# Softmax scalings and low parts of the early FFN from ScalarE and VectorE to GpSimd, with the weight pieces dealt out anew

## The chip, the cores and the metric

The kernel runs on one core of a Trainium2 chip. The metric is the device time of one execution in microseconds (us), as the median of several. The engines are named as in the profile: PE (TensorE, matrix products and transposes), PEld (its loading of weights), DVE (VectorE), ACT (ScalarE), POOL (GpSimd) and SP (SyncE, which only issues DMAs here).

## What is computed

Attention with a decay per key, 8 batches of 8 heads with 576 rows and 64 columns, and behind it a feed-forward network (FFN) on the 4608 × 512 output. All data are float32.

```python
def _attn_ref(q, k, v, f):
    scores = scale * np.matmul(q, k.transpose(0, 1, 3, 2))
    cum = np.cumsum(np.log(np.clip(f, 0.0001, 1.0)), axis=-1)
    decay = cum[:, :, :, None] - cum[:, :, None, :]
    scores = np.where(causal, -1000000000.0, scores + decay)
    attn = np.exp(scores - np.max(scores, axis=-1, keepdims=True))
    attn = attn / (np.sum(attn, axis=-1, keepdims=True) + 1e-09)
    return np.matmul(attn, v)

def _moe_ref(x, w_in, w_out):        # x: 4608 x 512, w_in: 512 x 2048, w_out: 2048 x 512
    h = x @ w_in
    return np.maximum(0.01 * h, h) @ w_out
```

## The kernel before

The large products are made of three: each operand is split into a high part in a rounded format that PE multiplies fast, and a low part, the rest; high by high, high by low and low by high are added up. So for the FFN the input has `xh` and `xl`, the weights `win_h`, `win_l`, `wout_h`, `wout_l`, and the activated hidden tile `g` has `gh` and `gl`.

The kernel has an early part and a main part. The **early part** (the loop over `steps`, some 140 us) handles the first 256 rows of three batches, 12 pairs of heads, four to a batch. At step x it issues, in this order: the loads of the next pair (`early_load`), the scores of pair x (`early_scores`), weight pieces up to the sum of `WQ[:x + 1]` (`load_weight`), the values of pair x − 1 (`early_values`), and so many quanta of the FFN as `FQ[x]` says (0 for the first four steps, then 4, then 8). The **main part** goes through the other rows head by head, with quanta of the FFN between its pieces; behind it the rest of the FFN runs alone.

*Scores of an early pair*: PE makes four score tiles `sce`, two of 128 and two of 256 columns. For each, DVE adds the causal mask and takes the maximum (L279, into `ze`), and ACT the exponential with the row sum (L283). Behind the last of them DVE prepares the reciprocal of the sums (L288, L289), and the four tiles are scaled by it (L291, an activation on ACT). *Values*: PE transposes `ze` (`tre`), ACT copies the result (`pte`, L303), PE multiplies with `ve` (`ave`), ACT writes `xh` (L316) and DVE `xl` (L317). The first FFN tile of a group of 256 rows needs `xh` and `xl` of all four pairs of its batch.

*A weight piece* (16 in all; even ones are two column blocks of `w_in`, odd ones of `w_out`) comes as packed 64-bit numbers: SP fetches it into `wraw` (L156; two buffers, so a fetch waits until the last step of the piece two before is done), ACT converts (L170), DVE shifts (L171), ACT rounds to the high part (L172), DVE masks, scales the rest, subtracts and adds (L173, L175, L179, L180), the last of which writes `win_l` or `wout_l`. Piece n is used by the FFN's column block n // 2.

*A quantum chain of the FFN* (`ffn`): 24 matmuls make `h` of 256 rows and 256 hidden columns, ACT makes `g` from it (L587), DVE `gh` (L590), and `gl` is `g − gh` (L592). In the main part POOL does `gl`, in the early part and in the last iteration DVE. In the next block's turn `second` multiplies `gh` and `gl` with `wout` into `o`. `qk`, `ve`, `g`, `gh` and `gl` share five buffers with the tag `b2`, so a new tile waits until the last reader of an older one is done.

The order of the instructions on each engine is fixed when the kernel is built: a scheduler takes the program's order and priorities and lays out one list for each engine, which the engine goes through in that order. So a change of the program can shift places in the lists of engines that it does not name.

Of the kernel before, what the change touches and what calls it, by code (L numbers as in the profile page):

```python
# [12 lines left out]
AF = mybir.ActivationFunctionType  # L13
ALU = mybir.AluOpType
# [8 lines left out]
B2 = 5  # L23
B4 = 4
NE = 3
WQ = (1, 1, 1, 1, 1, 1, 1, 1, 2, 2, 2, 2)
ZE = (("z0", "z1", "z2", "z3"), ("vm", "s2b", "m2b", "s2a"))
FQ = (0, 0, 0, 0, 4, 8, 8, 8, 8, 8, 8, 8, 8)
BUFS = dict(s1=2, m1=2, ost=2)
# [8 lines left out]
def forgetting_attention_ffn(ctx, tc, qT, kT, v4, vr, f, w_in, w_out, out):  # L38
# [6 lines left out]
    nc = tc.nc  # L45
# [23 lines left out]
    def width(i):  # L69
        return min((i + 1) * P, S)  # L70
# [32 lines left out]
    def matmul(*args, **kw):  # L103
        work[0] += 1
        nc.tensor.matmul(*args, **kw)  # L105
# [7 lines left out]
    def warm(n):  # L113

        ps = psum.tile([P, 512], F32, tag="h", name=f"warm_{len(warmed)}")
        warmed.append(n)
        for _ in range(n):
            matmul(ps, still[:, :P], still, start=True, stop=True)
# [66 lines left out]
    def weights(n):  # L185
        while len(loaded) < min(n, len(wpieces)):
            load_weight(len(loaded))
# [23 lines left out]
    for i in range(NCH):  # L211
        c = slice(i * P, width(i))
# [12 lines left out]
    def load(t):  # L225

        s, c0, c1 = tasks[t]
        h = state[t] = {}
        a, n = c0 * P, S
        for name, src, lo in (("q", qT, a), ("k", kT, 0)):  # L230
            x = h[name] = one.tile([P, S], F32, tag=f"{name}raw", name=f"{name}raw_{t}")
            for o in range(2):
                nc.sync.dma_start(x[o * D:(o + 1) * D, lo:n], src[s][:, lo:n])
        if s % 2 == 0:
            g = s // 2
            vm = fixed["vm"]
            nc.sync.dma_start(vm[:, :, :NFULL], v4[g])
            nc.sync.dma_start(vm[:REST, :, NFULL], vr[g])
            pairs[s // 2, c0] = {}
# [14 lines left out]
    def early_scores(b, g):  # L254
        e = early[b, g]
        mx = one.tile([P, 4], F32, tag="max", name=f"maxe_{b}_{g}", bufs=3)
        sm = one.tile([P, 4], F32, tag="sum", name=f"sume_{b}_{g}", bufs=3)
        for i in range(2):
            n = width(i)
            ps = [  # L260
                psum.tile([P, 512], F32, tag="sc", name=f"sce_{b}_{g}_{2 * o + i}")[:, :n]
                for o in range(2)
            ]
            for o in range(2):
                x = e["qk"][o * D:(o + 1) * D]
                matmul(ps[o], x[:, 0, i * P:n], x[:, 1, :n], start=True, stop=False)
            for o in range(2):
                s = b * HPB + 2 * g + o
                matmul(
                    ps[o], pick[:, s:s + 1].broadcast_to([P, P]), decay_r[i],  # L270
                    start=False, stop=True,
                )
            for o in range(2):
                c = 2 * o + i
                tag = ZE[g % 2][c]
                z = e[c] = one.tile(
                    [P, n], F32, tag=tag, name=f"ze_{b}_{g}_{c}", bufs=BUFS.get(tag, 1)
                )
                nc.vector.tensor_tensor_reduce(  # L279
                    out=z, in0=ps[o], in1=tri[:, TRI - n:], scale=-SCALE, scalar=3.0e38,  # L280
                    op0=ALU.add, op1=ALU.min, accum_out=mx[:, c:c + 1],
                )
                nc.scalar.activation(  # L283
                    z, z, AF.Exp, bias=mx[:, c:c + 1], scale=-1.0, accum_out=sm[:, c:c + 1]
                )
            if b * HPB // 2 + g < WARM[2]:
                warm(WARM[1])
        nc.vector.tensor_scalar(sm, sm, 1.0e-9, None, op0=ALU.add)  # L288
        nc.vector.reciprocal(sm, sm)  # L289
        for c in range(4):  # L290
            nc.scalar.activation(e[c], e[c], AF.Copy, scale=sm[:, c:c + 1])  # L291

    def early_values(b, g):
        e = early[b, g]
# [241 lines left out]
    since, done = {}, []  # L536
# [7 lines left out]
    def fetch_group(n):  # L544
        if n not in groups and n not in staged and (n + 1) * T <= ready[0]:
            xs = staged[n] = one.tile([P, NCC, T], F32R, tag="b4", name=f"xs_{n}", bufs=B4)
            since[n] = work[0]
            nc.sync.dma_start(xs.bitcast(F32), xd[:, n * T:(n + 1) * T].rearrange("(c p) t -> p c t", p=P))
# [8 lines left out]
    def ffn():  # L557
        pending = None
        half = NFC // 2
        order = [(0, 0, HP), (1, 0, HP), (0, HP, half), (1, HP, half)]  # L560
        order += [(n, 0, half) for n in range(2, NG)]
        for at, (n, p0, p1) in enumerate(order):
            while (n + 1) * T > ready[0]:
                yield False
            if n not in groups:
                if n not in staged:
                    fetch_group(n)
                while n not in groups:
                    yield False
            acc = [None, None]  # L570
            for p in range(p0, p1):
                while len(loaded) < 2 * (p + 1):
                    yield False
                xh, xl = groups[n]
                ph = psum.tile([P, 2, T], F32, tag="h", name=f"h_{n}_{p}")
                for e in range(2):
                    fs = slice(e * P, (e + 1) * P)
                    for c in range(NCC):
                        for x, (w, xx) in enumerate(((win_h[p], xh), (win_h[p], xl), (win_l[p], xh))):
                            matmul(  # L580
                                ph[:, e, :], w[:, c, fs], xx[:, c, :],
                                start=(c == 0 and x == 0), stop=(c == NCC - 1 and x == 2),
                            )
                    if e == 0:
                        yield True
                g = one.tile([P, 2, T], F32, tag="b2", name=f"g_{n}_{p}", bufs=B2)
                nc.scalar.activation(g, ph, AF.Prelu, alpha=0.01)  # L587
                gh = one.tile([P, 2, T], F32R, tag="b2", name=f"gh_{n}_{p}", bufs=B2)
                gl = one.tile([P, 2, T], F32R, tag="b2", name=f"gl_{n}_{p}", bufs=B2)
                nc.vector.tensor_copy(gh, g)  # L590
                eng = nc.gpsimd if heads[0] else nc.vector
                eng.tensor_tensor(gl, g, gh.bitcast(F32), op=ALU.subtract)  # L592
                yield True
                if pending is not None:
                    yield from second(*pending)
                if p0 < p and at + 1 < len(order):
                    fetch_group(order[at + 1][0])
                pending = (n, p, p0, p1, gh, gl, acc)
        yield from second(*pending)
# [27 lines left out]

    parts = {}
    quanta = ffn()
    heads = [False]  # L630
    ready, used, credit = [0], [0], [0.0]

    def fill(n):

        settle()
        credit[0] += n
        while credit[0] >= 1:
            credit[0] -= 1
            if not next(quanta, None):
                credit[0] = 0  # L640
                return
            used[0] += 1

    nt = len(tasks)
# [16 lines left out]
    for x, (b, g) in enumerate(steps + [(NE, 0)]):  # L661
        if x + 1 < len(steps):
            early_load(*steps[x + 1])
        if x < len(steps):
            early_scores(b, g)
            weights(sum(WQ[:x + 1]))
        if x:
# [5 lines left out]
    load(0)  # L673
    split(0)
    for t in range(nt + 1):
        heads[0] = t < nt
        if t + 1 < nt:
            load(t + 1)
        before = list(range(max(tasks[t - 1][1] - 1, 0), NCH)) if t else []
        now = list(range(*tasks[t][1:])) if t < nt else []  # L680
        have = ready[0] // T * NQ - used[0]
        left = min((e + 2 - t for e in ends if e + 1 >= t), default=1)
        step = min(have / (left + SLACK), MAXQ) / 8
        fill(step)
        for i in range(5):
            if i in before:
                transposes(t - 1, i)
            if i in now:
                scores(t, i)
            fill(step)  # L690
            if i == 1 and t and tasks[t - 1][0] % 2:
                inverse(t - 1)
        if t:
            for part in range(len(spans(t - 1))):
                values(t - 1, part)
                fill(step)
            if tasks[t - 1][0] % 2:
                normalise(t - 1)
            s, c0, c1 = tasks[t - 1]
            if s % HPB == HPB - 1:  # L700
                ready[0] = place[s // HPB, c0 * P] + S - c0 * P
        if t + 1 < nt:
            split(t + 1)
        fill(step * (3 - len(spans(t - 1)) if t else 1))
# [37 lines left out]
```

## Time and profile before

| what | value |
|---|---|
| time, median of 3 runs | 1215.92 us (1212.28 to 1219.12) |
| the profiled execution | 1216.96 us, span 1215.0 us, mean granted PE clock 0.993 |
| busy in the span | PE 1190.4 us (98%), DVE 623.4 (51%), ACT 628.6 (52%), POOL 467.9 (39%) |
| instructions | PE 7812, DVE 1682, ACT 1631, POOL 475 |

The profile shows one execution. Its rows give busy time and the idle time ahead of an instruction with what ended it. The span runs from the first to the last instruction; the time of the execution is 1.96 us longer. A group of instructions is shown as line, engine, operation, out<-in with the shapes, and their number; behind the bar stand the busy time and the mean ns of one, then the idle time before them and its releasers. In a timeline a row has start, duration, engine, line and operation; in brackets the idle time ahead and its releaser.

### The profile page before, as it was taken

How to read it: one execution, taken by the hardware profiler on the slowest of the kernel's cores; microseconds unless marked ns; L12 is line 12 of the kernel's file. 1: busy time of each engine (PE TensorE's matmuls, PEld its weight loads, DVE VectorE, ACT ScalarE, POOL GpSimd, SP SyncE). 2: the span in 40 equal slices, each digit the busy share in tenths (PEclk: the TensorE clock that was granted, in tenths of full speed). 3: DMA queues.
4: the chain of work that ended last, by engine and by line, in shares of the span. 5: the costliest groups of instructions: out<-in, count | busy, mean ns of one | idle time of the engine just before them, and what ended most of it. 6: DMA issues, size and time to landing. Idle time of an engine off the chain costs nothing.

```text
span 1215.0 us, 22228 instructions
## 1 busy us (share of the span) xinstructions
PE 1190.4 (98%) x7812; PEld 1070.4 (88%) x7812; DVE 623.4 (51%) x1682; ACT 628.6 (52%) x1631; POOL 467.9 (39%) x475
## 2 busy tenths in 40 slices
PE   8999989999999999999999999999999999999998
PEld 5678879888889999999999999999999999999997
DVE  6898556666645555455544444545444434553211
ACT  5876546667645565555545445454444444652111
POOL 2000255564455445454344453534454544531000
PEclk9899999999999999999999999999999999999999
DMA  6554233334333233323231322222223222211000
GB/s 193 168 192 165 83 103 110 95 104 140 107 106 97 79 97 97 114 80 92 83 109 51 89 80 90 73 90 61 75 84 90 60 69 81 72 57 47 18 18 18
DMA packets 81103, 110.53 MB, mean 91 GB/s; under 512 B 19616, under 2 KB 50704, under 8 KB 80992
## 3 DMA queue, kind: packets, MB, share of 16 engines
q1 hardware_dynamic: 80992, 109.11, 29.6%
q8 instruction: 62, 1.02, 0.3%
q14 instruction: 49, 0.40, 0.1%
HBM read 82.62 MB, written 18.58 MB: 83 GB/s over the span
## 4 chain that ended last, share of the span: by engine, by line
PE 86%; DVE 4%; ACT 3%; DMA 3%; issue 2%; POOL 1%; SPq 0%; ACTq 0%; POOLq 0%; DVEq 0%
PE h L105 32%; PE o L105 30%; PE tr L109 7%; PE av L105 7%; PE sc L105 7%; PE sce L105 1%; DMA kraw<-in_kT 1%; DMA wraw<-in_w_out 1%; ACT fixed_z L384 1%; PE ave L105 1%; DVE fixed_z L378 1%; DMA wraw<-in_w_in 1%; DVE pl L430 1%; DMA xd<-x 0%; DVE wraw L179 0%
## 5 line engine op out<-in xcount | busy, mean ns | idle before, releaser
L105 PE MATMUL h<-xh,win_h 128*128 128x256 f32 x1152 | 330.2, 287 | 0.3 <-ACT xh L316 0.3
L105 PE MATMUL h<-xh,win_l 128*128 128x256 f32 x1152 | 327.9, 285 | 0.0
L105 PE MATMUL h<-xs,win_h 128*128 128x256 f32 x1024 | 290.0, 283 | 4.0 <-POOL xs L143 4.0
L592 POOL TENSOR_TENSOR gl<-g,gh 128x512 fp32r<-128x512 f32 x111 | 146.9, 1324 | 290.9 <-DVE gh L590 269.0
L105 PE MATMUL o<-wout_h,gh 128*128 128x512 f32 x576 | 230.6, 400 | 0.0
L105 PE MATMUL o<-wout_l,gh 128*128 128x512 f32 x576 | 226.6, 393 | 0.0
L105 PE MATMUL o<-wout_h,gl 128*128 128x512 f32 x576 | 225.3, 392 | 0.0
L105 PEld LDWEIGHTS h<-xh,win_h 128*128 128x128 f32 x1152 | 220.7, 192 | 3.4 <-ACT xh L316 0.8
L105 PEld LDWEIGHTS h<-xh,win_l 128*128 128x128 f32 x1152 | 221.2, 192 | 0.7 <-issue 0.7
L384 ACT ACTIVATE fixed_z<-fixed_z,max 128x192 f32<-128x192 f32 (+3 forms) x272 | 161.0, 592 | 106.0 <-DVE max L378 102.4
L378 DVE CUSTOM_DVE_ANT_0 fixed_z<-sc,tri 128x192 f32<-128x192 f32 (+3 forms) x272 | 122.6, 452 | 159.3 <-PE sc L105 156.3
L105 PEld LDWEIGHTS h<-xs,win_h 128*128 128x128 f32 x1024 | 195.6, 191 | 6.6 <-POOL xs L143 4.6
L587 ACT ACTIVATE g<-h 128x512 f32<-128x512 f32 x144 | 85.8, 596 | 217.3 <-PE h L105 212.5
L428 ACT CAST ph<-tr 128x192 fp32r<-128x192 f32 (+3 forms) x360 | 126.4, 373 | 138.5 <-PE tr L109 98.6
L590 DVE CAST gh<-g 128x512 fp32r<-128x512 f32 x144 | 72.3, 502 | 209.4 <-ACT g L587 206.7
L430 DVE TENSOR_TENSOR pl<-tr,ph 128x384 fp32r<-128x384 f32 (+3 forms) x296 | 137.8, 467 | 76.2 <-ACT ph L428 75.7
L143 POOL TENSOR_TENSOR s<-qraw,s 64x576 fp32r<-64x576 f32 (+1 forms) x64 | 78.6, 1228 | 208.5 <-ACT s L347 208.5
L109 PE MATMUL tr<-ident_r,fixed_z 128*128 128x128 f32 x888 | 145.8, 274 | 7.3 <-DVE ph L435 2.4
L109 PEld LDWEIGHTS tr<-ident_r,fixed_z 128*128 128x128 f32 x888 | 107.4, 140 | 30.0 <-ACT rbr L508 5.0
L105 PEld LDWEIGHTS o<-wout_h,gl 128*128 128x128 f32 x576 | 108.2, 188 | 24.1 <-DVE maxe L279 0.4
L105 PEld LDWEIGHTS o<-wout_h,gh 128*128 128x128 f32 x576 | 108.7, 189 | 15.6 <-issue 0.3
L105 PEld LDWEIGHTS o<-wout_l,gh 128*128 128x128 f32 x576 | 108.8, 189 | 14.7
(108 smaller groups left out, 1731.9 us busy)
## 6 DMA issues: line engine op xcount, KB each, us to landing
kraw<-in_kT SPq DMA_DIRECT2D x128, 144.0 KB
qraw<-in_qT SPq DMA_DIRECT2D x80, 144.0 KB
wraw<-in_w_in SPq DMA_DIRECT2D x16, 512.0 KB
wraw<-in_w_out SPq DMA_DIRECT2D x16, 512.0 KB
fixed_vm<-in_v SPq DMA_DIRECT2D x32, 256.0 KB
xs<-xd SPq DMA_DIRECT2D x16, 512.0 KB
out<-ost SPq DMA_DIRECT2D x28, 256.0 KB
xd<-x SPq DMA_DIRECT2D x20, 288.0 KB
```

Source lines behind the costliest of these rows:

```text
L105: nc.tensor.matmul(*args, **kw)
L109: nc.tensor.transpose(*args)
L143: nc.gpsimd.tensor_tensor(out, a, b, op=ALU.subtract)
L378: nc.vector.tensor_tensor_reduce(out=z[:, a:b], in0=ps[:m, :b - a], in1=tri[:m, at:at + b - a], scale=-SCALE, scalar=3.0e38 if x == 0 else ...
L384: nc.scalar.activation(z, z, AF.Exp, bias=h["max"][:m, last:last + 1], scale=-1.0, accum_out=fixed["sum" + "ab"[s // 2 % 2]][:m, i, s % 2: ...
L428: nc.scalar.copy(strided(ph, run), source(ps, run))
L430: nc.vector.tensor_tensor(strided(pl, run), source(ps, run), strided(ph, run).bitcast(F32), op=ALU.subtract)
L587: nc.scalar.activation(g, ph, AF.Prelu, alpha=0.01)
L590: nc.vector.tensor_copy(gh, g)
L592: eng.tensor_tensor(gl, g, gh.bitcast(F32), op=ALU.subtract)
```

## The change

`WQ` deals the 16 pieces out otherwise: one each at the first and the second pair as before, none at the third and fourth, one each at the fifth and sixth, two each from the seventh pair on (before from the ninth on). The four scalings of a pair (L291, 48 in all) go from ACT to POOL as `tensor_scalar`. `gl` is made on POOL except behind the main loop, so 14 tiles of the early part and one in the last iteration go from DVE to POOL.

```diff
--- before.py
+++ after.py
@@ -23,7 +23,7 @@
 B2 = 5
 B4 = 4
 NE = 3
-WQ = (1, 1, 1, 1, 1, 1, 1, 1, 2, 2, 2, 2)
+WQ = (1, 1, 0, 0, 1, 1, 2, 2, 2, 2, 2, 2)
 ZE = (("z0", "z1", "z2", "z3"), ("vm", "s2b", "m2b", "s2a"))
 FQ = (0, 0, 0, 0, 4, 8, 8, 8, 8, 8, 8, 8, 8)
 BUFS = dict(s1=2, m1=2, ost=2)
@@ -288,7 +288,7 @@
         nc.vector.tensor_scalar(sm, sm, 1.0e-9, None, op0=ALU.add)
         nc.vector.reciprocal(sm, sm)
         for c in range(4):
-            nc.scalar.activation(e[c], e[c], AF.Copy, scale=sm[:, c:c + 1])
+            nc.gpsimd.tensor_scalar(e[c], e[c], sm[:, c:c + 1], None, op0=ALU.mult)
 
     def early_values(b, g):
         e = early[b, g]
@@ -588,7 +588,7 @@
                 gh = one.tile([P, 2, T], F32R, tag="b2", name=f"gh_{n}_{p}", bufs=B2)
                 gl = one.tile([P, 2, T], F32R, tag="b2", name=f"gl_{n}_{p}", bufs=B2)
                 nc.vector.tensor_copy(gh, g)
-                eng = nc.gpsimd if heads[0] else nc.vector
+                eng = nc.vector if done else nc.gpsimd
                 eng.tensor_tensor(gl, g, gh.bitcast(F32), op=ALU.subtract)
                 yield True
                 if pending is not None:
@@ -627,7 +627,6 @@
 
     parts = {}
     quanta = ffn()
-    heads = [False]
     ready, used, credit = [0], [0], [0.0]
 
     def fill(n):
@@ -673,7 +672,6 @@
     load(0)
     split(0)
     for t in range(nt + 1):
-        heads[0] = t < nt
         if t + 1 < nt:
             load(t + 1)
         before = list(range(max(tasks[t - 1][1] - 1, 0), NCH)) if t else []
```

The list of DVE, around the FFN's first cast `gh_0_0`. In names, the number behind `wraw` or `wt` is the weight piece, `ze_1_1_3` is tile 3 of batch 1, pair 1; `xl_0_173<-ave_0_3` is `xl` of batch 0 for its fourth pair. Before:

```order
L179 TENSOR_TENSOR wraw_4_516<-wt_4_519,win_h_2_95 128x1024
L317 TENSOR_TENSOR xl_0_173<-ave_0_3_539,xh_0_172 128x256
L180 TENSOR_TENSOR win_l_2_103<-wraw_4_516 128x1024
L279 ISA ze_1_1_3_641,maxe_1_1_613<-sce_1_1_3_633,tri_176 128x256
L279 ISA maxe_1_1_613 128x1
L171 TENSOR_SCALAR wt_5_658<-wt_5_658 128x1024
L288 TENSOR_SCALAR sume_1_1_614<-sume_1_1_614 128x4
L173 TENSOR_SCALAR wraw_5_655<-wt_5_658 128x1024
L590 CAST gh_0_0_573<-g_0_0_571 128x512
L289 RECIPROCAL sume_1_1_614<-sume_1_1_614 128x4
L175 SCALAR_TENSOR_TENSOR wraw_5_655<-wraw_5_655 128x1024
L592 TENSOR_TENSOR gl_0_0_574<-g_0_0_571,gh_0_0_573 128x512
```

And after the change:

```order
L179 TENSOR_TENSOR wraw_3_602<-wt_3_605,wout_h_1_110 128x1024
L289 RECIPROCAL sume_1_0_453<-sume_1_0_453 128x4
L317 TENSOR_TENSOR xl_0_173<-ave_0_3_517,xh_0_172 128x256
L279 ISA ze_1_1_0_568,maxe_1_1_560<-sce_1_1_0_562,tri_176 128x128
L279 ISA maxe_1_1_560 128x1
L279 ISA ze_1_1_2_571,maxe_1_1_560<-sce_1_1_2_563,tri_176 128x128
L279 ISA maxe_1_1_560 128x1
L180 TENSOR_TENSOR wout_l_1_118<-wraw_3_602 128x1024
L171 TENSOR_SCALAR wt_4_717<-wt_4_717 128x1024
L173 TENSOR_SCALAR wraw_4_714<-wt_4_717 128x1024
L590 CAST gh_0_0_551<-g_0_0_549 128x512
L279 ISA ze_1_1_1_585,maxe_1_1_560<-sce_1_1_1_579,tri_176 128x256
```

Before, `xl` for `ave_0_3` stands behind L179 of piece 4 and `gh_0_0` behind L173 of piece 5; after it, behind L179 of piece 3 and L173 of piece 4. `gl_0_0` is gone from this list.

The list of PE where the tile `gl_1_2` is first used (11th pair; `o_1_0<-wout_h_2,gl_1_2` is that use, `sce_2_2_3` the pair's last score). Before:

```order
L105 MATMUL sce_2_2_3_1274<-qk_2_2_1089 128x256
L105 MATMUL sce_2_2_1_1273<-both_146 128x256
L105 MATMUL sce_2_2_3_1274<-both_146 128x256
L109 MATMUL tre_2_1_0_1313<-ident_r_91,ze_2_1_1_1114 128x128
L109 MATMUL tre_2_1_1_1319<-ident_r_91,ze_2_1_2_1105 128x128
L109 MATMUL tre_2_1_1_1319<-ident_r_91,ze_2_1_3_1117 128x128 x2
L105 MATMUL h_0_4_1333<-xh_0_172,win_h_4_97 128x256
L105 MATMUL h_0_4_1333<-xl_0_173,win_h_4_97 128x256
L105 MATMUL h_0_4_1333<-xh_0_172,win_l_4_105 128x256
L105 MATMUL h_0_4_1333<-xh_0_172,win_h_4_97 128x256
L105 MATMUL h_0_4_1333<-xl_0_173,win_h_4_97 128x256
L105 MATMUL o_1_0_0_1075<-wout_h_2_111,gl_1_2_1196 128x512
```

And after the change, from the same score matmuls on:

```order
L105 MATMUL sce_2_2_3_1274<-qk_2_2_1089 128x256
L105 MATMUL sce_2_2_1_1273<-both_146 128x256
L105 MATMUL sce_2_2_3_1274<-both_146 128x256
L105 MATMUL ave_2_1_1325<-pte_2_1_0_1317,ve_2_1_922 64x256
L105 MATMUL o_1_0_0_1075<-wout_h_2_111,gl_1_2_1196 128x512
L105 MATMUL o_1_0_0_1075<-wout_h_2_111,gh_1_2_1195 128x512
```

Before, four transposes and five `h` matmuls stand between the last score and the use of `gl`; after it one `ave` matmul does, and the transposes and one `h` stand ahead of the scores.

The list of POOL from the last product `s` of the early part on, after the change; before, the list has no L291 and no L592 in this part, and goes from this `s` to the clearing of `fixed_z`:

```order
L143 TENSOR_TENSOR s1_1_1806<-qraw_1_1746,s1_1_1806 64x320
L291 TENSOR_SCALAR ze_1_0_0_460<-ze_1_0_0_460,sume_1_0_453 128x128
L291 TENSOR_SCALAR ze_1_0_1_477<-ze_1_0_1_477,sume_1_0_453 128x256
L291 TENSOR_SCALAR ze_1_0_2_463<-ze_1_0_2_463,sume_1_0_453 128x128
L291 TENSOR_SCALAR ze_1_0_3_480<-ze_1_0_3_480,sume_1_0_453 128x256
L592 TENSOR_TENSOR gl_0_0_552<-g_0_0_549,gh_0_0_551 128x512
L291 TENSOR_SCALAR ze_1_1_0_568<-ze_1_1_0_568,sume_1_1_561 128x128
L291 TENSOR_SCALAR ze_1_1_1_585<-ze_1_1_1_585,sume_1_1_561 128x256
L291 TENSOR_SCALAR ze_1_1_2_571<-ze_1_1_2_571,sume_1_1_561 128x128
L291 TENSOR_SCALAR ze_1_1_3_588<-ze_1_1_3_588,sume_1_1_561 128x256
L592 TENSOR_TENSOR gl_0_1_660<-g_0_1_657,gh_0_1_659 128x512
```

The four scalings of each early pair and the `gl` of the FFN alternate here.

## Prediction

> **What bounds the kernel now.** I first read the busy time by stretches of the span, since a share over the whole span mixes an early part with a long steady one. Columns: length, then busy time of PE, PEld, DVE, ACT and POOL, the granted PE clock, DMA share, GB/s.
>
> ```profile
> 20.00:62.00 42.00, 37.67 (x193) 27.36 (x193) 33.03 (x82) 34.10 (x93) 1.02 (x1) 0.84 0.55 180
> 62.00:160.00 98.00, 97.51 (x622) 80.67 (x621) 74.01 (x142) 58.65 (x135) 11.73 (x21) 1.00 0.47 153
> 200.00:1100.00 900.00, 890.76 (x5988) 816.14 (x5987) 453.35 (x1321) 487.07 (x1300) 420.62 (x415) 1.00 0.29 87
> ```
>
> From 62 us on PE is the bound: 97.51 of 98 us, then 890.76 of 900 us, at clock 1.00. The waits of PE between 62 and 160 us come to one line, 0.2 us:
>
> ```profile
> PE sce L105 <- DVE maxe L279: 0.2, 1, 0.2
> ```
>
> So the change, whose work ends near 140 us, can earn time only before 62 us, where PE is idle for 42.00 − 37.67 = 4.3 us and runs at 0.84. After that it can only lose. The timeline of PE shows the place: the first FFN tile waits for `xl` of the fourth pair.
>
> ```profile
> 51.90 0.50 PE L105 MATMUL h<-xh,win_h 128*128 128x256 f32 x2 [0.34 <-ACT xh L316]
> 53.23 0.39 PE L105 MATMUL h<-xl,win_h 128*128 128x256 f32 x1 [0.83 <-DVE xl L317]
> ...
> 62.10 0.50 PE L105 MATMUL o<-wout_h,gh 128*128 128x512 f32 x1
> 52.76 0.42 DVE L317 TENSOR_TENSOR xl<-ave,xh 128x256 fp32r<-128x256 f32 x1
> ```
>
> And a stretch of one microsecond shows the clock there (busy PE, clock, DMA share, GB/s):
>
> ```profile
> 56.00:57.00 1.00, 1.00 (x7) 0.50 0.90 307
> ```
>
> Right behind gaps of 0.34 and 0.83 us the clock is half, although PE is fully busy. By the durations of single `h` matmuls (0.41 us each instead of 0.28) the slow stretch runs from 53.7 to 57 us.
>
> [...]
>
> **Part 1, the weights.** One piece on DVE is L171 + L173 + L175 + L179 + L180 (mean ns of the early groups):
>
> ```profile
> L171 DVE TENSOR_SCALAR wt<-wt 128x1024 int32<-128x1024 int32 x14 | 9.6, 688 | 4.2 <-ACT wt L170 4.0
> L173 DVE TENSOR_SCALAR wraw<-wt 128x1024 int32<-128x1024 int32 x15 | 11.0, 732 | 0.3
> L175 DVE SCALAR_TENSOR_TENSOR wraw<-wraw 128x1024 f32<-128x1024 uint32 x15 | 18.3, 1220 | 0.1
> L179 DVE TENSOR_TENSOR wraw<-wt,wout_h 128x1024 f32<-128x1024 f32 x8 | 9.7, 1218 | 0.1
> L180 DVE TENSOR_TENSOR wout_l<-wraw 128x1024 fp32r<-128x1024 f32 x8 | 9.7, 1216 | 0.0
> L592 DVE TENSOR_TENSOR gl<-g,gh 128x512 fp32r<-128x512 f32 x10 | 6.8, 685 | 0.3 <-PE o L105 0.3
> L291 ACT ACTIVATE ze<-ze,sume 128x256 f32<-128x256 f32 x24 | 11.9, 498 | 0.0
> L291 ACT ACTIVATE ze<-ze,sume 128x128 f32<-128x128 f32 x24 | 9.5, 396 | 1.6 <-DVE sume L289 1.5
> ```
>
> 0.69 + 0.73 + 3 × 1.22 = 5.07 us. With no new pieces at the third and fourth pair, the fourth pair's `xl` stands behind L179 of piece 3, no longer of piece 4: 5.07 us less DVE work ahead of it. ACT also loses its burst of scalings, 2 × (0.40 + 0.50) = 1.8 us a pair, ahead of the exponentials and copies that the same pairs wait for. If the two gaps go (1.17 us) and the half clock (3.3 us at half speed cost 1.65) with them, PE's first second-layer matmul comes 5.1 + 1.8 + 1.2 + 1.65 = 9.7 us sooner at best. At least it is the 5.1 that `xl` no longer waits for. I take **8 us** (54.1 instead of 62.10): the gaps and the slow stretch hang on the late `xl` and go with it, ACT's burst I count at nothing, because `xl` stood behind DVE's own work. This is a lead, not yet a gain.
>
> **Part 2, the scalings on POOL.** No row of before has this operation there. The nearest are a one-input pass and a two-input subtract:
>
> ```profile
> L654 POOL TENSOR_SCALAR_AFFINE_SELECT tri<-tri 128x128 f32<-128x128 f32 x1 | 0.3, 292 | 0.0
> L143 POOL TENSOR_TENSOR fixed_vs<-fixed_vm,fixed_vs 128x320 fp32r<-128x320 f32 x64 | 64.7, 1012 | 16.2 <-ACT fixed_vs L356 9.0 <-POOL fixed_z L390 3.8 <-DMA qraw<-in_qT 1.1
> L592 POOL TENSOR_TENSOR gl<-g,gh 128x512 fp32r<-128x512 f32 x111 | 146.9, 1324 | 290.9 <-DVE gh L590 269.0 <-DMA rbr<-rows 13.3 <-DMA fixed_s2b<-dec_q 6.9
> ```
>
> Low end: 0.29 for either size, 1.2 us a pair. High end by the two-input row, 1.012 × 128/320 and × 256/320: 0.4 and 0.8, 2.4 us a pair. I take 0.30 and 0.50, 1.6 us a pair, near the one-input row, because a scaling reads one tile. Alone this costs nothing, since ACT's burst took 1.8 and POOL is idle (1.02 us busy of 42).
>
> **Part 3, gl on POOL.** DVE is rid of 15 × 0.685 us, POOL takes 15 × 1.32. Where `gl` has long been computed when PE asks, this is free. At three places it isn't: the tile of `gl` becomes free only with the last score of its pair, and PE wants it soon after. In before:
>
> ```profile
> 115.42 0.50 PE L105 MATMUL sce<-both 128*128 128x256 f32 x2
> 115.76 0.60 PE L109 MATMUL tre<-ident_r,ze 128*128 128x128 f32 x4
> 115.99 0.68 DVE L592 TENSOR_TENSOR gl<-g,gh 128x512 fp32r<-128x512 f32 x1
> 116.79 0.44 PE L105 MATMUL o<-wout_h,gl 128*128 128x512 f32 x1
> ```
>
> Four transposes and five `h` matmuls (115.76 to 116.79) cover DVE's 0.68. Now 1.32 us stand behind the same score, and at this pair only one `ave` matmul lies between (0.2 to 0.4 us): PE waits about 1.0 us. At the pair ahead of it and the one behind, the transposes still stand there (0.6), so 0.6 to 1.0. Bounds for all three: 1.2 us if a `gl` alone takes 1.0 us and the transposes cover it, 3.6 us if nothing does. I take **3 us**. The one `gl` that moves in the last iteration has main work beside it: nothing.
>
> **Part 4, DVE beside a busy POOL.** This is the unknown that decides. At the start, before shows both engines at once:
>
> ```profile
> 10.72 1.86 POOL L143 TENSOR_TENSOR both<-d,both 64x128 fp32r<-64x128 f32 x2 [8.60 <-ACT both L200]
> 12.54 2.41 POOL L143 TENSOR_TENSOR fck<-fc,fck 64x576 fp32r<-64x576 f32 x1
> 14.92 2.40 POOL L143 TENSOR_TENSOR fcq<-start,fcq 64x576 fp32r<-64x576 f32 x1
> 11.14 0.85 DVE L173 TENSOR_SCALAR wraw<-wt 128x1024 int32<-128x1024 int32 x1
> 12.03 1.64 DVE L175 SCALAR_TENSOR_TENSOR wraw<-wraw 128x1024 f32<-128x1024 uint32 x1
> 13.77 2.27 DVE L179 TENSOR_TENSOR wraw<-wt,win_h 128x1024 f32<-128x1024 f32 x1
> 16.07 0.29 DVE L279 CUSTOM_DVE_ANT_0 ze<-sce,tri 128x128 f32<-128x128 f32 x1
> 16.50 1.90 DVE L180 TENSOR_TENSOR win_l<-wraw 128x1024 fp32r<-128x1024 f32 x1
> ```
>
> DVE's weight steps took 0.12, 0.42, 1.05 and 0.68 us longer than their means, 2.27 us in all, beside 6.67 us of POOL; `ze`, which reads PSUM, took what it always takes. So DVE loses about 0.34 us for each us that POOL is busy, or nearly half of each us of POOL's undisturbed work (about 4.8 us, by 1.43 us for the same size when little stands beside it in later rows):
>
> ```profile
> L143 POOL TENSOR_TENSOR s<-qraw,s 64x576 fp32r<-64x576 f32 x40 | 57.0, 1426 | 112.2 <-ACT s L347 112.2
> ```
>
> Now piece 6, which `h_0_3` needs, by these rows:
>
> ```profile
> 56.91 0.43 DVE L590 CAST gh<-g 128x512 fp32r<-128x512 f32 x1 [0.27 <-ACT g L587]
> L279 DVE CUSTOM_DVE_ANT_0 ze<-sce,tri 128x256 f32<-128x256 f32 x22 | 8.6, 419 | 3.6 <-PE sce L105 3.5
> 74.90 0.39 PE L105 MATMUL h<-xh,win_l 128*128 128x256 f32 x1
> 114.23 0.29 DVE L279 CUSTOM_DVE_ANT_0 ze<-sce,tri 128x128 f32<-128x128 f32 x1 [1.25 <-PE sce L105]
> L170 ACT ACTIVATE wt<-wraw 128x1024 f32<-128x1024 f32 x14 | 16.1, 1151 | 10.6 <-DVE wraw L179 6.0 <-DVE win_l L180 2.9 <-DMA wraw<-in_w_out 1.7
> 94.35 0.69 DVE L171 TENSOR_SCALAR wt<-wt 128x1024 int32<-128x1024 int32 x1 [2.04 <-ACT wt L170]
> 92.38 6.17 DMA wraw<-in_w_out
> ```
>
> From the first `gh` through piece 6's last step DVE's order now holds 13.8 us of weight steps (three of piece 4, all of 5 and 6), four wide and four narrow `ze` (2.8), three `gh` (1.3), two `xl` (0.8) and small sums (0.7): 19.4 us. That `gh` comes 8 us sooner than at 56.91, at 48.9, so piece 6 is ready at 68.3 if nothing is lost. PE went from `o` to the first `win_l` of `h_0_3` in 74.90 − 62.10 = 12.8 us; the new order has a further half pair of scores and transposes in between, some 1.5 us by estimate from the same rows, so PE is there at 54.1 + 14.3 = 68.4: just in time. POOL's work in this stretch, three scalings and two `gl`, is 7.4 us; at full price DVE is at 74 to 75, and PE loses 6 to 7 of its 8 us; at half price 3.
>
> The fetches are moved as well. SP issues them in order, that of piece 6 behind the loads of the seventh pair (which wait for a tile that POOL's first `gl` reads) and behind piece 4's last step. A fetch takes 6.17 us and ACT's step 1.15; piece 4 ends near 54.6, so ACT is done at 61.9 and DVE gets to L171 at 62.3. No wait, but no room either; before had one of 2.04 us at such a place, and that much is the price if the fetch comes late.
>
> Later, pieces 7, 8 and 9 stand ahead of `ze` of the tenth pair with nothing but a few short steps between them; by the same durations it comes 10 us sooner than in before at no loss, and level with before at full price. From there each pair brings 1.6 + 2 × 1.32 us of POOL and relieves DVE of 1.4: at full price 2.9 us later per pair less the idle time that DVE has there (1.25 us at 114.23), 1.6 us, and over two pairs 3.
>
> **Sum.** Without any loss on DVE: −8 + 3 = **−5 us**. At full price: −8 + 8 + 3 = **+3 us** (this 3 is the lateness of the last two pairs, which holds the waits for `gl`). At half price, which the start's rows are nearest to: **−1 us**. The profiled execution took 1216.96 us (span 1215.0 and 1.96 around it), 1.04 over the median of 1215.92, and stands inside 1212.28 to 1219.12. 1216.96 − 1 = 1216.
>
> **The rivals.** (a) *The lead is kept.* POOL works mostly while DVE reads PSUM or waits (DVE has 24 us idle between 62 and 160), so weights are not late. For it: the steady part runs POOL at 47% beside DVE with no harm to PE. Against it: DVE's weight steps are long and back to back just where POOL's bursts fall. −5 us, or with the full 9.7 and waits of 1.2 us −8.5: 1208.5 to 1212.
>
> (b) *Slower: every two-input DVE step and every POOL instruction exclude each other.* Place: pieces 6 to 11, 60 to 115 us. Price: the +3 above, and each wait of PE over some 0.8 us then brings half clock for 3.3 us, 1.65 us a time as at 53.7 us; one to three times, 1220 + 1.65 to 5 = 1221.5 to 1225. The kernel is slower from the point at which DVE loses more than 5/8 = 0.63 us for each us of POOL's undisturbed work, where the −5 is eaten. For it: L179 at 2.27 instead of 1.22. Against it: that row was the worst of four.
>
> [...]
>
> (c) *The change doesn't act*: the FFN does not start sooner because the fourth pair's chain through `tre`, `pte` and `ave` was late anyway. `xl` at 52.76 followed L179 with no wait of its own, which speaks against it. The lead would then be 3 us instead of 8: −1 + 5 = 4, 1220.
>
> **Chances.** Forecast, half price, 1214 to 1219.5: 0.5. (a) 0.23, (b) 0.2, (c) 0.07. Predicted 1216; the range from 1208.5, the best of (a), to 1223, within (b). A measurement of this kernel can tell about 0.5% (6.1 us) from no change: faster means under 1209.8, slower over 1222. Most of (a) lies within that, so faster 0.18; of (b) some 0.6, with measurement spread 0.16 for slower; same 0.66.
>
> **What would show it.** Right: first second-layer matmul near 54 us; L291 on POOL at 0.3 to 0.5 us; L175, L179, L180 at 1.3 to 1.6 us instead of 1.22; a wait of PE for `win_l` near 68 to 71 us and three waits for POOL's `gl` between 90 and 130; the main part reached about 1 us sooner. (a) would show L175 to L180 still at 1.22 and no wait for `win_l`; (b) steps near 2 us, waits of 5 us, and clock 0.5 behind 62 us. Wrong altogether: L291 on POOL near 1 us each, so that `tre` waits for it at every pair, or a change in the part behind 160 us.

## The result

The change makes the kernel slower: 1230.29 us (median of 4, 1229.45 to 1233.81) against 1215.05 us, a ratio of 1.0129 with a 95% interval of 1.0104 to 1.0155. The profiled execution took 1233.81 us (span 1231.9), 16.85 us more than that of before; it is the slowest of the four. The forecast was 1216 us, 1208.5 to 1223.

The busy time by stretches after the change; columns as in the prediction:

```profile
20.00:62.00 42.00, 36.91 (x182) 23.81 (x181) 26.89 (x72) 24.52 (x71) 25.26 (x23) 0.84 0.44 142
62.00:160.00 98.00, 89.71 (x534) 70.49 (x534) 75.39 (x134) 50.38 (x105) 58.06 (x42) 0.97 0.42 139
200.00:1100.00 900.00, 891.20 (x5978) 816.39 (x5978) 455.52 (x1327) 490.24 (x1306) 426.72 (x420) 1.00 0.30 89
```

The steady part is as before (891.20 of 900 us, 890.76 before). Behind 62 us PE, which was idle for 0.5 us of 98, is now idle for 8.3, and its clock is 0.97. Ahead of 62 us nothing was won: PE is busy for 36.91 us, and the clock is 0.84 again. A mark for the whole is the first mask step of the main part on DVE, before and after:

```profile
161.22 0.48 DVE L378 CUSTOM_DVE_ANT_0 fixed_z<-sc,tri 64x320 f32<-64x320 f32 x1 [2.64 <-PE sc L105]
```

```profile
177.46 0.48 DVE L378 CUSTOM_DVE_ANT_0 fixed_z<-sc,tri 64x320 f32<-64x320 f32 x1 [3.36 <-PE sc L105]
```

It comes 16.2 us later, and the span behind it is nearly the same (1215.0 − 161.22 = 1053.8, now 1054.4). So the loss lies in the early part. From 20 us on to this mark PE is idle for 13.4 us instead of 4.8, which is 8.6 of the 16.2 us; the rest is lower clock and longer PE work. What PE waits for there, between 20 and 160 us (us in all, times, longest):

```profile
PE tre L109 <- POOL ze L291: 8.2, 10, 1.6
PE sce L105 <- DVE maxe L279: 3.3, 2, 2.6
PE o L105 <- POOL gl L592: 1.4, 3, 0.9
```

The first line is new: the transposes wait for the scalings on POOL. POOL's groups in the same stretch:

```profile
L291 POOL TENSOR_SCALAR ze<-ze,sume 128x256 f32<-128x256 f32 x24 | 34.7, 1448 | 0.0
L291 POOL TENSOR_SCALAR ze<-ze,sume 128x128 f32<-128x128 f32 x24 | 28.5, 1187 | 27.3 <-DVE sume L289 16.8 <-DVE maxe L279 9.1 <-PE ave L105 1.4
L592 POOL TENSOR_TENSOR gl<-g,gh 128x512 fp32r<-128x512 f32 x11 | 16.8, 1530 | 25.0 <-PE sce L105 16.3 <-DVE sume L288 8.7
```

A scaling takes 1.19 and 1.45 us where the sum had 0.30 and 0.50: 5.27 us a pair instead of 1.6. The timeline of PE shows what such a wait brings with it (start, duration, in brackets the wait):

```profile
23.51 0.33 PE L109 MATMUL tre<-ident_r,ze 128*128 128x128 f32 x1 [1.11 <-POOL ze L291]
25.14 0.91 PE L109 MATMUL tre<-ident_r,ze 128*128 128x128 f32 x3 [0.24 <-POOL ze L291]
27.59 0.69 PE L109 MATMUL tre<-ident_r,ze 128*128 128x128 f32 x2 [1.54 <-POOL ze L291]
28.20 0.79 PE L105 MATMUL sce<-qk 64*128 64x128 f32 x2
28.93 1.54 PE L105 MATMUL ave<-pte,ve 128*64 128x256 f32 x4
...
63.61 0.40 PE L105 MATMUL o<-wout_h,gh 128*128 128x512 f32 x1
```

```profile
27.00:28.00 1.00, 0.41 (x2) 0.50 0.84 174
30.00:31.00 1.00, 1.00 (x5) 0.50 0.01 4
33.00:34.00 1.00, 1.00 (x5) 0.50 0.00 0
```

PE waits three times within five us, and from 27 us, while the third wait still lasts, to 34 us at least its clock is half: four `ave` matmuls take 1.54 us, where four take 0.86 at 37 us. The FFN's first `o` comes at 63.61, later than before's 62.10, not at 54.1.

### The profile page after: what moved, and what is told of

Read it like the earlier page. It is cut to its first block, busy times and chain, and to the rows that moved or that the text cites. A ratio compares the mean times of both kernels' runs of the same rounds, so it can differ in the third digit from the quotient of the medians.

```text
span 1231.9 us, 22273 instructions
## 1 busy us (share of the span) xinstructions
PE 1198.9 (97%) x7812; PEld 1071.9 (87%) x7812; DVE 621.5 (50%) x1667; ACT 614.5 (50%) x1583; POOL 551.5 (45%) x538
## 4 chain that ended last, share of the span: by engine, by line
PE 84%; POOL 4%; DMA 4%; ACT 3%; DVE 2%; issue 2%; SPq 1%; ACTq 0%; POOLq 0%; DVEq 0%
PE h L105 31%; PE o L105 29%; PE tr L109 7%; PE av L105 7%; PE sc L105 6%; POOL ze L291 2%; PE sce L105 1%; DMA wraw<-in_w_in 1%; DMA kraw<-in_kT 1%; PE ave L105 1%; POOL gl L592 1%; ACT fixed_z L384 1%; DVE fixed_z L378 0%; DMA xd<-x 0%; PE tre L109 0%
## 5 line engine op out<-in xcount | busy, mean ns | idle before, releaser
L592 POOL TENSOR_TENSOR gl<-g,gh 128x512 fp32r<-128x512 f32 x126 | 169.1, 1342 | 329.1 <-DVE gh L590 280.2
```

## The experiments

Ratios are to the kernel before on the same chip, with their 95% intervals. The clock is the lowest and the highest mean PE clock that was granted to an execution of the run; the kernel before had 0.984 to 0.999 beside these runs, 0.995 on average.

| run | table | scalings | gl of the early part | median us | ratio (interval) | clock |
|---|---|---|---|---|---|---|
| the change | new | POOL, column | POOL | 1230.29 | 1.0129 (1.0104 to 1.0155) | 0.989 to 0.994 |
| e1 | old | POOL, column | DVE | 1240.82 | 1.0199 (1.0146 to 1.0252) | 0.976 to 0.986 |
| e2 | new | ACT | DVE | 1216.04 | 1.0010 (0.9985 to 1.0035) | 0.991 to 0.997 |
| e3 | new | ACT | POOL | 1223.00 | 1.0067 (1.0039 to 1.0095) | 0.985 to 0.995 |
| e4 | old | ACT | POOL | 1221.81 | 1.0060 (1.0037 to 1.0082) | 0.991 to 0.996 |
| e6 | new | POOL, column | DVE | 1221.24 | 1.0052 (1.0023 to 1.0081) | 0.990 to 0.998 |
| e7 | new | half ACT, half POOL | POOL | 1227.88 | 1.0088 (1.0062 to 1.0115) | 0.986 to 0.996 |
| e8 | new | DVE | DVE | 1218.93 | 1.0033 (1.0005 to 1.0062) | 0.993 to 0.999 |
| e9 | new | ACT | first 6 on POOL | 1222.97 | 1.0061 (1.0033 to 1.0089) | 0.986 to 0.994 |
| e10 | new | ACT | later 8 on POOL | 1216.71 | 1.0007 (0.9987 to 1.0028) | 0.991 to 0.998 |
| e11 | milder | ACT | DVE | 1216.79 | 1.0003 (0.9979 to 1.0027) | 0.989 to 0.997 |
| e12 | new | POOL, two tiles | POOL | 1224.79 | 1.0066 (1.0043 to 1.0090) | 0.988 to 0.996 |
| e17 | new | POOL, two tiles | DVE | 1215.45 | 1.0015 (0.9999 to 1.0030) | 0.991 to 0.998 |
| e18 | new | POOL, two tiles | later 8 on POOL | 1226.44 | 1.0096 (1.0076 to 1.0115) | 0.988 to 0.992 |

### One part at a time: e1 to e4

e1 is the kernel before with this alone:

```diff
-            nc.scalar.activation(e[c], e[c], AF.Copy, scale=sm[:, c:c + 1])
+            nc.gpsimd.tensor_scalar(e[c], e[c], sm[:, c:c + 1], None, op0=ALU.mult)
```

> Only the scalings (L291) go to POOL; weights and gl as before. Theory A (the scalings are slow on POOL, 5.3 us a pair instead of ACT's 1.8, and each pair's transposes wait for them): slower than before by 8 to 18 us, PE waits for POOL ze of 5 us or more in all. Theory B (gl on POOL and DVE locked out by it): within 4 us of before. Theory C (weight pieces dealt out later come too late): within 4 us of before.

e2 is the kernel before with the new table alone:

```diff
-WQ = (1, 1, 1, 1, 1, 1, 1, 1, 2, 2, 2, 2)
+WQ = (1, 1, 0, 0, 1, 1, 2, 2, 2, 2, 2, 2)
```

> Only the weight table changes. A and B: between 6 us faster and 3 us slower than before, since less DVE work stands ahead of the fourth pair's xl. C: slower by 8 to 15 us, with PE waiting for win_l or DVE behind schedule near 65 to 120 us.

e3 is the changed kernel with e1's line taken back:

```diff
-            nc.gpsimd.tensor_scalar(e[c], e[c], sm[:, c:c + 1], None, op0=ALU.mult)
+            nc.scalar.activation(e[c], e[c], AF.Copy, scale=sm[:, c:c + 1])
```

> The changed kernel with the scalings back on ACT: new weight table and gl on POOL stay. A: 1208 to 1217 us, the first second-layer matmul at 53 to 57 us. B or C: 1225 us or more.

e4 is e3 with the old table, so `gl` alone:

```diff
-                eng = nc.gpsimd if heads[0] else nc.vector
+                eng = nc.vector if done else nc.gpsimd
```

> Only gl goes to POOL; table and scalings as before. A and C: within 4 us of before, with up to 3 us of waits for POOL gl. B: slower by 8 us or more.

The scalings alone cost 2.0%, more than the whole change; `gl` alone 0.6%; the table nothing. Part of this is clock. An execution's time, multiplied by what its clock lacked of 1.00, estimates what half clock cost it: on average 5.8 us in before's 25 executions beside e1, 11.4 in the change, 22.6 in e1. So some 17 of e1's 25 us, and 6 of the change's 15, would be half clock and not waiting. Theory C falls (e2), and neither A nor B stands alone: A was right on e1 and on what e3 gives back (1230.29 to 1223.00), B on the 7 us that e3 and e4 keep. In e2 the row of the first `o` and the mark of the main part are:

```profile
51.77 0.40 PE L105 MATMUL o<-wout_h,gh 128*128 128x512 f32 x1
...
157.80 0.48 DVE L378 CUSTOM_DVE_ANT_0 fixed_z<-sc,tri 64x320 f32<-64x320 f32 x1 [2.64 <-PE sc L105]
```

The first `o` is 10.3 us sooner than before, the main part only 3.4 us. The stretches from 20 us to the first `o`, and from there to the mark, in before and then in e2:

```profile
20.00:62.10 42.10, 37.77 (x194) 27.36 (x194) 33.03 (x82) 34.20 (x93) 1.02 (x1) 0.84 0.55 180
62.10:161.22 99.12, 98.63 (x631) 81.88 (x630) 74.02 (x143) 58.55 (x135) 12.22 (x21) 1.00 0.47 151
```

```profile
20.00:51.77 31.77, 31.44 (x189) 22.61 (x189) 20.88 (x70) 28.52 (x88) 0.00 (x0) 0.96 0.48 145
51.77:157.80 106.03, 104.09 (x639) 84.25 (x638) 85.66 (x156) 66.66 (x144) 12.99 (x22) 1.00 0.51 163
```

Of the 10.3 us, 4.0 are idle time that is gone, 5.4 are half clock (0.84 of 42.10 us, 0.96 of 31.77), and under 1 is less work: in the whole list ahead of the first `o` only eight `ave` matmuls are missing (250 records instead of 258). The clock's part is a matter of the execution that was profiled: before's had 0.993 and e2's 0.997, but their timed executions have 0.995 on average, both of them. Behind the first `o` e2 needs 6.9 us more to the mark: 1.5 us of idle time and 5.5 us of busy PE, with only those eight `ave` more (0.14 us each in before, so about 1.1). Why the same matmuls take some 4 us longer there at full clock is open.

### Why a scaling takes so long: e5, e7, e12

e5 is the kernel before with POOL instructions on a tile of ones added behind the main part:

```diff
+    for w in (P, 2 * P):
+        for _ in range(4):
+            nc.gpsimd.tensor_scalar(probe[:, :w], probe[:, :w], probe[:, 511:512], None, op0=ALU.mult)
+            nc.gpsimd.tensor_scalar(probe[:, :w], probe[:, :w], 1.0, None, op0=ALU.mult)
+            nc.gpsimd.tensor_tensor(probe[:, :w], probe[:, :w], probe[:, 256:256 + w], op=ALU.mult)
```

> The kernel before, with 24 extra POOL instructions on a tile of ones behind the main part, where DVE has little to do: a multiplication by a column's value, one by a constant, and one of two tiles, each four times at 128x128 and four times at 128x256. Theory A1 (the scaling itself is slow on POOL, whatever DVE does): 1.0 us or more for 128x128 by a column's value. [...] If the column's value alone is what costs, the constant is much quicker.

Single instructions of its timeline, a column's value (L710), a constant (L711), two tiles (L712), and DVE's beside one of them:

```profile
1093.83 0.46 POOL L712 TENSOR_TENSOR probe<-probe 128x128 f32<-128x128 f32 x1
1094.38 0.60 POOL L710 TENSOR_SCALAR probe<-probe 128x128 f32<-128x128 f32 x1
...
1100.03 0.85 POOL L711 TENSOR_SCALAR probe<-probe 128x256 f32<-128x256 f32 x1
1100.96 0.72 POOL L712 TENSOR_TENSOR probe<-probe 128x256 f32<-128x256 f32 x1
1101.78 0.92 POOL L710 TENSOR_SCALAR probe<-probe 128x256 f32<-128x256 f32 x1
...
1105.72 1.76 POOL L710 TENSOR_SCALAR probe<-probe 128x256 f32<-128x256 f32 x1
```

```profile
1105.06 1.10 DVE L592 TENSOR_TENSOR gl<-g,gh 128x512 fp32r<-128x512 f32 x1
1106.09 0.68 DVE L553 CAST xh<-xs 128x1024 fp32r<-128x1024 f32 x1
```

Alone a scaling takes 0.60 and 0.92 us, 3.04 a pair: twice the 1.6 of the prediction, over its high end of 2.4, and under the 1.0 that A1 set for 128x128. The remaining 5.27 − 3.04 = 2.2 us a pair come beside DVE's work: at 1105.72 the same instruction takes 1.76 us while DVE has a subtraction of two tiles (1.10 us, elsewhere 0.69) and a cast. The change's own trace shows the same two values: four of its 24 long scalings overlap with no weight step, no cast and no subtraction of DVE, and take 0.92 us each; fifteen overlap with one of the steps L175, L179 and L180, which read two tiles, and take 1.71 us on average. So A1 falls, though a good part is POOL's own time: of the 3.7 us a pair that the sum missed, 1.4 are that and 2.2 were lost beside DVE. The product of two tiles is the quicker form. e12 is the changed kernel with it:

```diff
-            nc.gpsimd.tensor_scalar(e[c], e[c], sm[:, c:c + 1], None, op0=ALU.mult)
+            nc.gpsimd.tensor_tensor(e[c], e[c], sm[:, c:c + 1].broadcast_to(list(e[c].shape)), op=ALU.mult)
```

> The changed kernel with the scaling written as a product of two tiles, the sums broadcast along the row: alone it took 0.46 and 0.73 us instead of 0.60 and 0.92. If POOL's own time per pair sets the loss: 0.66 us less a pair, 1225 to 1229 us against 1230.3. [...]

Its groups of POOL:

```profile
L291 POOL TENSOR_TENSOR ze<-ze,sume 128x256 f32<-128x256 f32 x24 | 23.6, 982 | 0.0
L291 POOL TENSOR_TENSOR ze<-ze,sume 128x128 f32<-128x128 f32 x24 | 19.1, 798 | 26.2 <-DVE sume L289 22.9 <-PE sce L105 1.9 <-PE ave L105 1.4
```

3.56 us a pair, and PE waits for them for 0.2 us in all. The median falls by 5.5 us, a little more than expected, and the ratio to that of e3 with the scalings on ACT. e7 is the changed kernel with the two short scalings of a pair on ACT:

```diff
-            nc.gpsimd.tensor_scalar(e[c], e[c], sm[:, c:c + 1], None, op0=ALU.mult)
+            if c % 2:
+                nc.gpsimd.tensor_scalar(e[c], e[c], sm[:, c:c + 1], None, op0=ALU.mult)
+            else:
+                nc.scalar.activation(e[c], e[c], AF.Copy, scale=sm[:, c:c + 1])
```

> The changed kernel, but the two 128x128 scalings of a pair stay on ACT and only the two 128x256 ones are on POOL. Theory A (POOL's time per pair is what the transposes wait for): between the 1223.0 us with all on ACT and the 1230.3 us with all on POOL, 1225 to 1228 us. If any POOL scaling costs the same whatever its length, 1230 us.

Its median lies between e3 and the change, as theory A has it, though the intervals overlap. e8 is e2 with all four on DVE:

```diff
-            nc.scalar.activation(e[c], e[c], AF.Copy, scale=sm[:, c:c + 1])
+            nc.vector.tensor_scalar(e[c], e[c], sm[:, c:c + 1], None, op0=ALU.mult)
```

> The new table, the scalings on DVE (some 0.2 us each by the other one-input passes there), gl on DVE as before. If ACT's bursts are in the way of the early pairs and DVE has room: 1209 to 1214 us. If DVE's order is the limit behind 62 us: 1216 to 1222 us, since 48 x 0.2 us come on top.

DVE takes 0.29 and 0.35 us for them, a quarter of POOL's time, and the result is the second of the two expected: nothing is gained over ACT. That DVE's order is the reason isn't shown.

### What the parts do to each other: e6 and e17

e6 is e1 with e2's table:

> The new table and the scalings on POOL, gl as before. If the costs of gl (7 us alone) and of the scalings (24 us alone) add up, about 1215 + 15.7 - 7 = 1224 us. If the gl on POOL gives back DVE time that the slow scalings need, about 1230 us or more.

e17 is e6 with e12's line in the place of e1's:

> The new table, scalings on POOL as products of two tiles, gl on DVE. If the form is what costs: 1213 to 1218 us, as the table alone, against 1221.2 with the column form. If any scaling on POOL costs: 1219 us or more.

PE's waits for the scalings between 20 and 160 us, in e1, e6, e12 and e17:

```profile
PE tre L109 <- POOL ze L291: 8.2, 11, 1.5
PE tre L109 <- POOL ze L291: 5.2, 7, 1.6
PE tre L109 <- POOL ze L291: 0.2, 1, 0.2
PE tre L109 <- POOL ze L291: 0.9, 4, 0.3
```

The scalings cost 24 us beside the old table (e1) and about 5 beside the new one (e6). The waits differ by 3 us only; most of the difference is half clock, 22.6 us against 6.6 by the estimate above (in the profiles the clock between 40 and 62 us is 0.66 and 1.00). A reason may be the missing weight pieces: the fourth pair's scalings take 5.9 us in e1 and 4.1 in e6, but the third pair's 3.8 and 4.0, so this isn't shown. With the quick form they cost nothing beside the new table (e17). e6 and `gl` (6 and 7 us) come near the change's 15, and e6 stays under both of its expected figures, so its "gives back" is refuted.

### Which gl cost: e9, e10, e13 to e16

e9 and e10 are e2 with the early `gl` split. e9, the first six on POOL:

```diff
-                eng = nc.gpsimd if heads[0] else nc.vector
+                eng = nc.gpsimd if heads[0] or n == 0 and p < HP or n == 1 and p < 2 else nc.vector
```

> The new table, scalings on ACT, and only the first six early gl on POOL (up to the first two blocks of the second batch); the later eight stay on DVE. Theory D (gl on POOL costs where PE asks for it right behind a pair's last score, in the later pairs): as the new table alone, 1213 to 1217 us. [...]

e10, the later eight on POOL, and the one of the last iteration:

```diff
-                eng = nc.gpsimd if heads[0] else nc.vector
+                eng = nc.vector if done or not heads[0] and (n == 0 and p < HP or n == 1 and p < 2) else nc.gpsimd
```

> The complement: the first six early gl on DVE, the later eight and the one in the last iteration on POOL. D: 1221 to 1224 us, as with all of them. [...]

The first six cost all of it, the later ones nothing, against D, and against an even share of the fourteen tiles in the 7 us. Some of the 7 us is clock again: by the estimate half clock cost e3 10.0 us and e9 10.7, e2 6.5 and e10 6.2. SP's waits between 40 and 160 us hold a line in e9 that e2 and e10 do not have:

```profile
SPq L248 <- POOL gl L592: 8.9, 3, 4.6
```

With L252 SP waits 12.0 us for POOL's `gl` in e9, where it waits 9.6 us for DVE's `gl` at such loads in e2; so the wait isn't new, but longer. The loads of the next pairs (L248, L252) reuse buffers that `gl` holds or reads, and the weight fetches queue behind these loads. In e9 the last step (L180) of piece 11 starts at 119.1 instead of 111.5 in e2, and PE waits 2.16 us at 97.92 for a DVE that has itself waited 2.38 us for ACT's conversion of a late piece. e13 to e16 give the loads of the first eight pairs buffers of their own. Theory F is that `gl` costs through SP's loads, G that it costs in another way:

```diff
-        x = e["qk"] = one.tile([P, 2, T], F32, tag="b2", name=f"qk_{b}_{g}", bufs=B2)
+        own = b * HPB // 2 + g < 8
+        tag, m = (f"part{g % 2}", 1) if own else ("b2", B2)
+        x = e["qk"] = one.tile([P, 2, T], F32, tag=tag, name=f"qk_{b}_{g}", bufs=m)
...
-        v = e["v"] = one.tile([P, 2, T // P, D], F32, tag="b2", name=f"ve_{b}_{g}", bufs=B2)
+        tag, m = ("ost", 2) if own else ("b2", B2)
+        v = e["v"] = one.tile([P, 2, T // P, D], F32, tag=tag, name=f"ve_{b}_{g}", bufs=m)
```

> Control: the new table alone, with the loads of the first eight early pairs (qk, ve) in buffers of their own, idle then, instead of the five shared with g, gh and gl. F and G: 1213 to 1218 us, since nothing on POOL is waited for; every load may come a little sooner.

> The same with the first six gl on POOL. F: SP no longer waits for POOL gl, and the time is within 3 us of the control. G: 5 to 8 us over the control, as e9 stands to the table alone.

> The full change with the same early buffers. F: 5 to 8 us less than 1230.3, so 1222 to 1225 us, the rest being the scalings. G: 1228 us or more.

> Control and try: the kernel before with the same early buffers. Before, SP's fetches wait for DVE's steps and not for loads, so no gain: 1212 to 1218 us.

| run | base | median us | ratio (interval) |
|---|---|---|---|
| e13 | e2 | 1218.31 | 1.0032 (1.0011 to 1.0054) |
| e14 | e9 | 1221.51 | 1.0046 (1.0025 to 1.0066) |
| e15 | the change | 1232.66 | 1.0136 (1.0102 to 1.0169) |
| e16 | before | 1217.47 | 1.0013 (0.9996 to 1.0029) |

The six `gl` now add 0.14% (e14 over e13) instead of 0.5% (e9 over e2), as F has it; but the control rose, and the intervals of e13 and e14 overlap, and SP still waits 3.0 us for POOL's `gl` in e14; so the path through SP is made likely and not shown. For the whole change F fails: e15 is no faster. In it SP still waits 12.3 us for POOL's `gl`, at the loads that kept the shared buffers, so the test of the change is not a clean one.

### Without the two dear parts: e18, and e11

e18 is e17 with e10's line, so two parts that cost nothing singly:

> The same with the later eight early gl and the one of the last iteration on POOL: the change without its two dear parts. If both parts were what cost: 1212 to 1218 us. Faster than before by over 0.5% is not expected, since the table alone was not.

It costs 1.0%, and the expectation fails. The rows of e17 and of e18, 20 to 62 us (from left PE, PEld, DVE, ACT, POOL, clock):

```profile
20.00:40.00 20.00, 19.52 (x98) 12.25 (x97) 15.63 (x46) 14.78 (x47) 8.94 (x13) 0.92 0.62 183
40.00:62.00 22.00, 21.52 (x138) 15.99 (x140) 20.10 (x44) 14.58 (x37) 12.13 (x13) 1.00 0.55 180
```

```profile
20.00:40.00 20.00, 18.71 (x84) 11.20 (x82) 13.32 (x39) 12.47 (x40) 7.44 (x11) 0.83 0.55 164
40.00:62.00 22.00, 20.65 (x122) 15.27 (x122) 17.79 (x42) 13.40 (x36) 11.46 (x14) 0.92 0.49 153
```

In this stretch both kernels have the same instructions in the same order on every engine, and yet e18's first `o` comes at 60.66 us instead of 55.16: in e18 a wait of 0.89 us for a scaling at 24.1 us is followed by half clock from 27 to 33 us, in e17 the clock is whole there and half from 20 to 23 only. The later loss is another: SP waits 8.3 us for one of the later `gl`, and PE is idle for 3.8 us between 120 and 140. The clock isn't the chance of one execution: all four of e18 (1223.59 to 1228.32) had 0.988 to 0.992, e17's ten 0.991 to 0.998, and by the estimate half clock cost them 12.3 and 5.8 us, so some 6 of the 11 us between the two are clock. Whether it falls early each time, and what the later `gl` has to do with it, stays open, as one of the four is profiled.

e11 is the kernel before with a milder table:

```diff
-WQ = (1, 1, 1, 1, 1, 1, 1, 1, 2, 2, 2, 2)
+WQ = (1, 1, 0, 1, 1, 1, 1, 2, 2, 2, 2, 2)
```

> The kernel before with a milder table: none at the third pair only, two each from the eighth on, 1 1 0 1 1 1 1 2 2 2 2 2. If the lead of the new table is lost because too many weight pieces stand behind 62 us, this keeps more of it: 1209 to 1213 us. If what was gained ahead of the FFN was only work put off, 1213 to 1217 us.

No difference: the milder table wins nothing either. No version beats the kernel before.

## Why the prediction was wrong

**What bounds, and where the change can act: right.** All of the loss lies ahead of the main part, and PE is the bound behind it. Against the sum of −8 + 4 + 3 = −1 us the ratios give +1 for the table alone (e2), 7 more with `gl` (e3) and 7.5 more with the scalings. So the lead was missed by 9 us, `gl` by 4 and the scalings by 7.5, and the 4 us set for DVE's loss are not needed beside them.

**Part 1, a lead of 8 us: right in time of the first `o`, failed as a lead.** Without the scalings `o` came at 51.77 (e2) and 53.02 (e3), sooner than the 54.1 of the sum. But the sum took the start of `o` for progress of PE. Only 3.4 of e2's 10.3 us reach the main part in its profile, and the timed runs show none. Half of the 10.3 is half clock that before's profiled execution happened to have; and between `o` and the main part e2 loses 6.9 us again with nothing on POOL, where the sum let only POOL's work eat the lead. Two of its smaller sums are off by about a microsecond, which changes nothing: 68.3 + 7.4 is 75.7 and not 74 to 75, and rival (c) comes to 1221.

**Part 2, the scalings at 1.6 us a pair, "Alone this costs nothing": this is the step that failed, with the lead of part 1.** They measured 5.27 us a pair, of which 3.04 is POOL's own time (e5) and the rest comes beside DVE's work, and cost 7.5 us (the change over e3). The bounds, 1.2 and 2.4, came from a pass without a column operand and from a two-tile subtract; the operation has a price of its own that no row of before shows, so the range should have gone well beyond both. The prediction's last sentence named the sign, "L291 on POOL near 1 us each, so that `tre` waits for it at every pair", and gave it no chance and no time. That the price acts through the transposes is shown by e12 and e17: with the quick form PE's wait goes from 8.2 us in the change to 0.2 (e12), and from 5.2 in e6 to 0.9 (e17), and the excess over e3 and over e2 goes with it. The waits come at some pairs, up to 83 us, and not at every pair.

That a scaling comes near the one-input row because it reads one tile was the author's estimate, and e5 is against it: on POOL, 0.92 us for one tile and a column's value is more than 0.72 for two tiles. Between the engines, the `gl` of before, with two tiles, took 1.32 us on POOL and 0.69 on DVE, 1.9 times as long; the scaling of 128x256 took 0.92 on POOL alone (e5) and 0.35 on DVE (e8), 2.6 times as long.

**Part 3, gl at 3 us: mis-sized and misplaced.** It measured 7 us (e3, e4). PE's waits for POOL's `gl` come to 3.2 us in e3, as the sum had them, so the rest comes another way. The later tiles, with the three places that the sum priced, cost nothing by themselves (e10, where PE waits 0.7 us); the six tiles that it called free cost all (e9), likely through SP's loads. The prediction did see that the seventh pair's load waits for POOL's first `gl`, and put it at "No wait, but no room either".

**Part 4, who pays when both run: the wrong engine.** The sum had DVE lose half of each us that POOL works. Two of DVE's groups in the change, 20 to 150 us, and the second of them in before:

```profile
L175 DVE SCALAR_TENSOR_TENSOR wraw<-wraw 128x1024 f32<-128x1024 uint32 x14 | 20.0, 1427 | 0.2
L180 DVE TENSOR_TENSOR win_l<-wraw 128x1024 fp32r<-128x1024 f32 x7 | 10.2, 1458 | 0.0
```

```profile
L180 DVE TENSOR_TENSOR win_l<-wraw 128x1024 fp32r<-128x1024 f32 x7 | 8.5, 1221 | 0.1
```

They lose 0.21 and 0.24 us each, 14 and 7 times, 4.6 us in all; the steps that write `wout_l` lose 0.5 us more, and L179 is nearly where it was. POOL loses 2.2 us in each of 12 pairs, 27 us. The engine that was thought to be idle anyway paid, and it stood on the path of the transposes. The full price counted a scaling like a `gl`, and no run shows that: in e6, with 62.6 us of scalings on POOL and `gl` on DVE, L175, L179 and L180 took 1.9 us more in all than in before.

In two overlaps the instruction that began second took much longer than elsewhere: POOL's scaling 1.76 us instead of 0.92 at 1105.72 in e5, when DVE's subtraction had begun at 1105.06, and DVE's L175 2.20 us instead of 1.22 at 133.82 in the change, when POOL's `gl` had begun at 133.25. The one that began first was longer too, 1.10 us instead of 0.69 and 1.68 instead of 1.32, so how the two engines share the time is not shown:

```profile
133.25 1.68 POOL L592 TENSOR_TENSOR gl<-g,gh 128x512 fp32r<-128x512 f32 x1 [3.69 <-DVE sume L288]
133.82 2.20 DVE L175 SCALAR_TENSOR_TENSOR wraw<-wraw 128x1024 f32<-128x1024 uint32 x1
```

**The rivals.** The sign was that of (b), its place too late and its price too small: what came late was less DVE than the scalings, from the first pair on. That DVE's steps and POOL's instructions exclude each other was its supposition, and no run shows it. Its other mechanism, half clock behind short waits, is in the profile (27 to 34 us), and comes with the transposes' waits. (c), a lead that is not there, is what the table alone shows in the timed runs, but not for the reason that (c) gave.

## What to carry to other kernels

An operation that the profile does not hold on an engine should get a range that reaches several times its nearest row, and its latency be laid along the path of whoever reads the result, even where the engine is idle. A marker that comes sooner in one profile is not yet time won: compare the clock of the two profiled executions with that of the timed ones, and look at a second marker further on. Where PE waits often, half clock can cost more than the waits themselves (e1: some 17 us of 25 by the estimate). Parts of such a change do not add up (24 us or 5 us for the same scalings, by the table beside them), so each is tried alone and in the company that it will have.

## What the runs showed of the hardware

POOL's product with a column's value (0.60 us for 128x128, 0.92 for 128x256) is slower than its product of two tiles (0.46 and 0.72), and a constant lies between (0.53 and 0.85; all e5). Beside DVE's work the column form took up to 2.73 us for one instruction of the change:

```profile
L291 POOL TENSOR_SCALAR ze<-ze,sume x48: 600/1257/2726, 22.8 to 156.1; 128x128 f32<-128x128 f32 x24, 128x256 f32<-128x256 f32 x24
```

With a repeated column as its second operand the product of two tiles took 0.80 and 0.98 us on average beside DVE's work (e12), where the column form took 1.19 and 1.45 (the change). Of products with 256 columns, one of rounded parts took 0.28 us on average (`h<-xl,win_h`, 128x128 weights) and one of plain float32 0.41 (`ave`, 128x64 weights), in before from 62.1 to 161 us at clock 1.00. And the same lists gave two early clocks, 0.92 and 0.83 between 20 and 40 us (e17 and e18).
